# First loads, w_in in parts, whole-batch q and k, and where P is normalised: a reordering of the start of a chunk-attention and gated feed-forward kernel

## The chip, the cores and the metric

The kernel runs on one core of a Trainium2 chip. The metric is the device time of one execution in microseconds (us). The core has a matrix engine (TensorE, PE in the profile, with its weight loads as PEld), a vector engine (VectorE, DVE), a scalar engine (ScalarE, ACT), GpSimd (POOL) and a sync engine (SyncE, SP). Each works through its own queue in program order. Loads and stores are DMAs, issued here from the queues of GpSimd, SP and ACT.

## What is computed

```python
B, H, S, D = 8, 8, 576, 64            # q, k, v: float32
chunk = 64                            # 9 chunks of 64 tokens
scores = (1 / sqrt(D)) * q_c @ k_c^T  # within each chunk
attn = softmax(scores)
attn_out = attn @ v_c
x = attn_out.transpose(0, 2, 1, 3).reshape(4608, 512)
h = x @ w_in                          # 512 x 2048
g = h * sigmoid(beta * h)             # beta: one per column
out = g @ w_out                       # 2048 x 512, float32 out
```

## The kernel before

All matmuls are in float16. Attention goes by **units**: batch 0 (in `WIDE`) has units of 4, 4 and 1 chunks (units 0, 1, 2), every other batch three units of 3 chunks (3 to 23). In one unit, both head halves of all chunks go through: turns of q and k on VectorE (`turn`, 32 x 32 block transposes, L197 and L206), scores on PE (`scores`, L249), row maximum (L261) and subtraction (`shift`, L270) on VectorE, exp on ACT (L278), row sum and reciprocal on VectorE (L289, L293), the product with the reciprocal that makes P (`norm`, L305 and L311), the transposition of P (`flip_pe` L325 with a copy by ACT L333 for the first nine units, `flip_dma` after), P times v on PE (`values`, L353 and L365), and the copy of the result into `XT` (`put`, L376; for units 0 and 1 half on VectorE L386 and half on ACT L384), which holds x transposed, 128 x 4 x 4608.

For units 0 and 1 the loads put 8 tokens of a head in one partition's row, and v is brought into order by matmuls with a selection matrix (`select`, L218; `sel` is made by `make_selectors`, L174 and L178, from an identity made on GpSimd) and copied out of the accumulators by ACT (`select_copy`, L229).

The feed-forward goes by blocks j of 512 tokens: 16 pieces of 128 columns of h (`m_mm`, L399, four matmuls each), tanh on ACT (L411), the gate on VectorE (L417), and then for each 128 tokens 16 matmuls with w_out (`t_mm`, L427), a copy by ACT (L437) and a store (L449, L455). Blocks 0 to 2 take their first step in two parts of tokens (`PIECES`), block 0 in two of 256.

The order of the instructions on every engine is fixed at build time by a planner (L460 to L730): each step is a task with an engine, a length, the tasks it waits for and the buffer slots it takes and gives; the planner puts out whatever can start soonest, feed-forward against attention by small penalties. `order` holds pairs that must keep their order. Loads on GpSimd (`pool`, L498) form one chain in the order of `LOADS` (L485) and then batch by batch; the planner lets one start when its model of the descriptor room (`RING`) has space.

Loads before: q of the first four chunks as float32 by SP and ACT (`load_first`, L137, four DMAs each, cast by VectorE L145 and ACT L143); all else by GpSimd, which casts to float16 on the way. That is k, v of the first four chunks (`load_wide`, L113), the identity, then q, k, v of the next four, w_in in two halves (L163), the first quarter of w_out (L168), the last chunk of batch 0 (`load_last`, L124 and L128), three quarters of w_out, batch 1 by heads in two parts (`load_pair`, L158 for q and k, L153 for v, 8 DMAs each), and the other batches by heads, 8 DMAs for each of q, k and v. P of units 0 to 6 is made on VectorE (`ON_DVE`, L480), of the others on GpSimd.

Of the kernel before, what the change touches and what calls it, by code (L numbers as in the profile page):

```python
# [16 lines left out]
def kernel(  # L17
# [20 lines left out]

    nc = tc.nc
# [9 lines left out]
    WIDE = (0,)  # L49
# [9 lines left out]
    NEARLY = sum(1 for u in units if u[0] in WIDE)  # L59
    first = {b: min(u for u in range(NU) if units[u][0] == b) for b in range(B)}  # L60
# [14 lines left out]
    w_in16 = big.tile([128, 2, KDM, DFF // 2], FP16)  # L75
# [34 lines left out]
    def load_wide(name, b, part):  # L110

        for x in range(2):
            nc.gpsimd.dma_start(  # L113
                out=wide_part(name, b, part)[:, x, :], in_=wide_src(name, b, x, part * 4 * CH))

    def load_last(name, b):

        f = raw_tile(name, b)[:, 2048:2304]
        t0 = 8 * CH
        for x in range(2):  # L120
            if name == "v":
                o = f[64 * x:64 * x + 64].rearrange("p (y s d) -> p y s d", y=2, s=2)
                for y in range(2):
                    nc.gpsimd.dma_start(  # L124
                        out=o[:, y],
                        in_=v[b, 4 * y + 2 * x:4 * y + 2 * x + 2, t0:t0 + CH].rearrange("s p d -> p s d"))
            else:
                nc.gpsimd.dma_start(  # L128
                    out=f[:, 128 * x:128 * x + 128],
                    in_=heads(name, b, x)[:, t0:t0 + CH, :].rearrange("r (p i) d -> r p (i d)", p=32))  # L130
# [15 lines left out]

    def load_pair(name, b, h, c0, n):

        i = srcs[name][b, h, c0 * CH:(c0 + n) * CH]
        if name == "v":  # L150
            p, y, s = 64 * (h // 2 % 2), h // 4, h % 2
            f = raw_tile(name, b).rearrange("p (c y s d) -> p c y s d", c=NCH, y=2, s=2)
            nc.gpsimd.dma_start(  # L153
                out=f[p:p + 64, c0:c0 + n, y, s], in_=i.rearrange("(c p) d -> p c d", p=CH))
        else:
            p, x = 32 * (h // 2), h % 2
            f = raw_tile(name, b).rearrange("p (c x e) -> p c x e", c=NCH, x=2)
            nc.gpsimd.dma_start(  # L158
                out=f[p:p + 32, c0:c0 + n, x], in_=i.rearrange("(c p i) d -> p c (i d)", p=32, i=2))

    def load_w_in(half):
        wv = moe_w_in.rearrange("(kk p) (a f) -> p a kk f", p=128, a=2)
        nc.gpsimd.dma_start(out=w_in16[:, half], in_=wv[:, half])  # L163
# [6 lines left out]
    def make_selectors():  # L170


        for g in range(4):
            nc.vector.tensor_copy(  # L174
                out=diag[32 * g:32 * g + 32], in_=ident[32 * g:32 * g + 32, 32 * g:32 * g + 32])
        for e in range(8):
            for y in range(2):
                nc.vector.tensor_copy(  # L178
                    out=sel[:, y, e].rearrange("p (c k) -> p c k", c=2)[:, :, 8 * e:8 * e + 8],
                    in_=diag[:, 16 * y:16 * y + 16].rearrange("p (c t) -> p c t", c=2))  # L180
# [5 lines left out]
    def turn(name, u, ss=(0, 1)):  # L186
# [3 lines left out]
        if grp is not None:  # L190
            if c0 % 4 == 0:
                f = raw[name, b][:, grp * 1024:grp * 1024 + 1024].bitcast(FP32)
                if 0 in ss:
                    tr[name, b, grp] = tr_p.tile([128, 4, 2, CH, 2], FP16, tag=name + "t", name=name + "t")
# [4 lines left out]
                    in_=f.rearrange("p (s j l) -> p (s j) l", s=2, j=8)[:, 8 * s0:8 * s0 + 8 * n_s])  # L199
            return  # L200
# [25 lines left out]
    def select_copy(b, grp, g):  # L226
        if g == 0:
            tr["v", b, grp] = vv_p.tile([128, 4, 2, 2, D], FP16, tag="vv", name="vv")
        nc.scalar.activation(  # L229
            out=tr["v", b, grp].rearrange("p g y x d -> p g (y x d)")[:, g],  # L230
            in_=sc["v", b, grp][g][:, 0:256], func=ACTF.Copy)
# [7 lines left out]
    def scores(u):  # L239
        n = units[u][2]  # L240
        x = ps_s.tile([128, 2, 512], FP32, tag="s", name="s")
        sc[u] = x
        for c in range(n):
# [53 lines left out]
    def norm(u, gs, eng):  # L297

        n, grp = units[u][2:]
# [8 lines left out]
        else:  # L308
            pn = sm_p.tile([128, m, 2, n, CH], FP16, tag="pn", name="pn")
            for s in range(2):  # L310
                eng.tensor_tensor(  # L311
                    out=pn[:, :, s], in0=ex.rearrange("p g (c s) k -> p s g c k", s=2)[:, s],
                    in1=rb.rearrange("p g (c s) o -> p s g c o", s=2)[:, s].broadcast_to([128, m, n, CH]), op=ALU.mult)
        pr[u, gs] = pn

    def flip_pe(u, gs):
# [6 lines left out]
        f = pn.rearrange("p e g k -> p (e g k)" if grp is None else "p g s c k -> p (g s c k)")  # L323
# [17 lines left out]
    def values(u):  # L341
# [4 lines left out]
        a = ps_x.tile([128, 2, 512], FP32, tag="x", name="xa")  # L346
        if grp is None:
            f = raw["v", b].rearrange("p (c y s d) -> p c y s d", c=NCH, y=2, s=2)
            for c in range(n):
                for y in range(2):  # L350
                    for s in range(2):
                        for g in range(2):
# [3 lines left out]
                                rhs=x[64 * g:64 * g + 64, 2 * c + s, 64 * y:64 * y + 64],  # L356
                                start=True, stop=True)
        else:
            for g in range(2):
                for y in range(2):  # L360
                    for c in range(2):
                        for s in range(2):
                            for r in range(2):
                                o = ((2 * y + g) * 2 + c) * CH
                                nc.tensor.matmul(  # L365
                                    out=a[64 * s:64 * s + 64, r, o:o + CH],
# [5 lines left out]
    def put(u, r=None):  # L372
# [8 lines left out]
        o = XT[:, :, t0:t0 + w].rearrange("p k (c r t) -> p k c r t", c=2, r=2)[:, :, :, r]  # L381
        i = xa[u][:, r].rearrange("p (k c t) -> p k c t", k=KDM, c=2)
# [10 lines left out]
    def m_mm(j, m, a, n):  # L393
# [4 lines left out]
        for kk in range(KDM):  # L398
            nc.tensor.matmul(  # L399
                out=hps[:, 0:n],  # L400
                lhsT=w_in16[:, kg // 2, kk, kg % 2 * 512 + i:kg % 2 * 512 + 512:4],
# [42 lines left out]
    def t_store(j, t):  # L444
# [6 lines left out]
        for i in range(2):  # L451
# [10 lines left out]
            "qt": 3, "kt": 3, "vv": 2}  # L462
# [298 lines left out]
```

## Time and profile before

| what | value |
|---|---|
| median of 3 runs | 318.75 us (318.69 to 320.44) |
| the profiled execution, its own time | 318.93 us |
| its span, first to last instruction | 316.9 us |
| PE, DVE, ACT, POOL busy | 285.8, 207.3, 176.0, 161.7 us |
| feed-forward matmuls L399 and L427 busy | 145.2 and 141.4 us |
| scores L249, transposes L325 busy | 14.6 and 5.3 us |
| P on GpSimd (17 units of 768 columns) | 25.2 us, 1.48 each |
| HBM read, written | 36.71 MB, 9.44 MB |

The profile is one execution. A line of its timeline gives start and length in us, the engine, the line of the kernel, the operation, output and inputs, how many were merged, and in brackets the idle time of that engine just before with what ended it. In a table of stages each engine's busy time stands with its count of instructions, and behind them the clock granted to TensorE as a share of full speed, the mean number of DMA engines' work as a share, and the rate in GB/s of what was written. The page's slices are a fortieth of the span each (7.9 us).

### The profile page before, as it was taken

How to read it: one execution, taken by the hardware profiler on the slowest of the kernel's cores; microseconds unless marked ns; L12 is line 12 of the kernel's file. 1: busy time of each engine (PE TensorE's matmuls, PEld its weight loads, DVE VectorE, ACT ScalarE, POOL GpSimd, SP SyncE). 2: the span in 40 equal slices, each digit the busy share in tenths (PEclk: the TensorE clock that was granted, in tenths of full speed). 3: DMA queues.
4: the chain of work that ended last, by engine and by line, in shares of the span. 5: the costliest groups of instructions: out<-in, count | busy, mean ns of one | idle time of the engine just before them, and what ended most of it. 6: DMA issues, size and time to landing. Idle time of an engine off the chain costs nothing.

```text
span 316.9 us, 7899 instructions
## 1 busy us (share of the span) xinstructions
PE 285.8 (90%) x3254; PEld 165.0 (52%) x3254; DVE 207.3 (65%) x378; ACT 176.0 (56%) x299; POOL 161.7 (51%) x239
## 2 busy tenths in 40 slices
PE   0358787799898999999999999999999999999995
PEld 0347447376684667655455555554444444444442
DVE  3666847589898888978978888887334434334300
ACT  1337455267775777667556866667644454544511
POOL 7624389999999968899689841113000000000000
PEclk9997999999999799999999999999999999999999
DMA  6999948999999999999999963222111000001011
GB/s 100 167 212 131 204 66 71 136 137 129 175 120 155 103 63 125 165 177 131 52 199 147 134 71 85 67 64 48 43 62 41 33 33 35 33 33 68 33 66 66
DMA packets 95315, 31.54 MB, mean 100 GB/s; under 512 B 87600, under 2 KB 88880, under 8 KB 95280
## 3 DMA queue, kind: packets, MB, share of 16 engines
q0 software_dynamic: 77184, 18.12, 60.4%
q10 hardware_dynamic: 5376, 9.70, 9.1%
q1 hardware_dynamic: 12720, 3.22, 7.6%
q8 instruction: 25, 0.41, 0.6%
q14 instruction: 10, 0.08, 0.1%
HBM read 36.71 MB, written 9.44 MB: 146 GB/s over the span
## 4 chain that ended last, share of the span: by engine, by line
PE 75%; DMA 12%; POOL 7%; DVE 2%; ACT 1%; issue 1%; ACTq 0%; DVEq 0%; POOLq 0%
PE hps L399 36%; PE ops L427 35%; DMA w_out<-in_moe_w_out_dram 8%; DMA kr<-in_k_dram 3%; POOL kr L158 3%; PE s L249 3%; PE xa L353 2%; POOL qr L158 2%; POOL vr L153 2%; DVE mx L261 1%; DVE sh L270 1%; POOL w_in L163 0%; PE pt L325 0%; ACT XT L376 0%; ACT osb L437 0%
## 5 line engine op out<-in xcount | busy, mean ns | idle before, releaser
L411 ACT ACTIVATE sg<-hps,beta_sb 128x512 f32<-128x512 f32 (+3 forms) x192 | 108.5, 581 | 77.5 <-PE hps L399 74.9
L399 PE MATMUL hps<-XT,w_in 128*128 128x512 f16 (+3 forms) x768 | 145.2, 332 | 5.7 <-ACT XT L384 2.8
L417 DVE SCALAR_TENSOR_TENSOR gt<-sg,hps 128x512 f16<-128x512 f32 (+3 forms) x192 | 104.8, 551 | 69.7 <-ACT sg L411 67.9
L427 PE MATMUL ops<-w_out,gt 128*128 128x512 f16 x576 | 141.4, 379 | 0.0
L399 PEld LDWEIGHTS <-w_in 128*128 128x128 f16 x768 | 84.6, 115 | 52.7 <-issue 6.3
L427 PEld LDWEIGHTS <-gt 128*128 128x128 f16 x576 | 55.1, 98 | 59.4
L153 POOL DMA_DIRECT2D vr<-in_v_dram x64 | 45.6, 763 | 0.0
L305 POOL TENSOR_TENSOR pn<-ex,ri 128x768 f16<-128x768 f16 x17 | 25.2, 1483 | 35.2 <-ACT sg L411 15.8
L158 POOL DMA_DIRECT2D qr<-in_q_dram x64 | 38.4, 650 | 6.6 <-DMA w_out<-in_moe_w_out_dram 5.8
L158 POOL DMA_DIRECT2D kr<-in_k_dram x64 | 37.9, 623 | 1.9 <-DMA qr<-in_q_dram 1.8
L437 ACT ACTIVATE osb<-ops 128x512 f32<-128x512 f32 x36 | 21.5, 597 | 28.8 <-PE ops L427 28.4
L249 PE MATMUL s<-kt,qt 32*64 32x64 f16 x1152 | 14.6, 197 | 15.2 <-DVE kt L197 10.8
L261 DVE TENSOR_REDUCE mx<-s 128x12 f32<-128x768 f32 (+3 forms) x25 | 22.8, 914 | 7.4 <-PE s L249 7.4
L289 DVE TENSOR_REDUCE sum<-ex 128x12 f32<-128x768 f16 (+3 forms) x25 | 22.5, 901 | 4.3 <-ACT ex L278 4.2
L270 DVE TENSOR_TENSOR sh<-s,mx 128x768 f32<-128x768 f32 (+3 forms) x25 | 22.7, 911 | 0.1
L278 ACT ACTIVATE ex<-sh 128x768 f16<-128x768 f32 (+3 forms) x25 | 20.2, 814 | 2.9 <-issue 0.8
L249 PEld LDWEIGHTS <-qt 32*64 32x64 f16 x1152 | 12.1, 111 | 18.4 <-DVE qt L197 10.1
L376 ACT ACTIVATE XT<-xa 128x768 f16<-128x768 f32 (+1 forms) x22 | 17.2, 782 | 2.4 <-PE xa L353 2.0
L206 DVE STREAM_TRANSPOSE kt<-kr 128x384 f32<-128x384 f32 (+1 forms) x22 | 12.0, 544 | 4.7 <-DMA kr<-in_k_dram 2.9
L333 ACT ACTIVATE et<-pt 128x768 f16<-128x768 f16 (+3 forms) x10 | 7.3, 744 | 10.6 <-PE pt L325 10.2
L206 DVE STREAM_TRANSPOSE qt<-qr 128x384 f32<-128x384 f32 (+1 forms) x22 | 12.0, 550 | 0.4 <-DMA qr<-in_q_dram 0.4
L325 PE MATMUL pt<-ident,pn 128*128 128x128 f16 x54 | 5.3, 232 | 6.4 <-DVE pn L311 4.5
(38 smaller groups left out, 69.6 us busy)
## 6 DMA issues: line engine op xcount, KB each, us to landing
out_dram<-osb ACTq DMA_DIRECT2D x32, 256.0 KB
qr<-in_q_dram POOLq DMA_DIRECT2D x48, 72.0 KB, 4.1
kr<-in_k_dram POOLq DMA_DIRECT2D x48, 72.0 KB, 3.4
vr<-in_v_dram POOLq DMA_DIRECT2D x48, 72.0 KB, 3.3
w_in<-in_moe_w_in_dram POOLq DMA_DIRECT2D x2, 1024.0 KB, 12.4
w_out<-in_moe_w_out_dram POOLq DMA_DIRECT2D x4, 512.0 KB, 9.0
out_dram<-osb ACTq DMA_DIRECT2D x8, 128.0 KB
kr<-in_k_dram POOLq DMA_DIRECT2D x4, 128.0 KB, 7.3
```

The source lines that it names most:

```text
L153: nc.gpsimd.dma_start(out=f[p:p + 64, c0:c0 + n, y, s], in_=i.rearrange("(c p) d -> p c d", p=CH))
L158: nc.gpsimd.dma_start(out=f[p:p + 32, c0:c0 + n, x], in_=i.rearrange("(c p i) d -> p c (i d)", p=32, i=2))
L206: nc.vector.transpose(out=o, in_=f.rearrange("p (e i l) -> p e i l", i=2, l=32))
L249: nc.tensor.matmul(out=x[p0:p0 + 64, r % 2, e:e + CH], lhsT=operand("q", u, r, s, h, c), rhs=operand("k", u, r, s, h, c), start=(h == 0), ...
L261: nc.vector.tensor_reduce(out=mx[:, 0:n].rearrange("p g e o -> p g (e o)"), in_=x[:, gs[0]:gs[-1] + 1, 0:E * CH].rearrange("p g (e k) -> p ...
L270: nc.vector.tensor_tensor(out=sh, in0=x[:, gs[0]:gs[-1] + 1, 0:E * CH].rearrange("p g (e k) -> p g e k", k=CH), in1=mx[:, 0:n].broadcast_t ...
L289: nc.vector.tensor_reduce(out=sm[:, 0:n * E].rearrange("p e o -> p (e o)"), in_=ex.rearrange("p g e k -> p (g e) k"), axis=AX.X, op=ALU.add)
L305: eng.tensor_tensor(out=pn.rearrange("p e g k -> p g e k"), in0=ex, in1=rb.broadcast_to([128, m, 2 * n, CH]), op=ALU.mult)
L399: nc.tensor.matmul(out=hps[:, 0:n], lhsT=w_in16[:, kg // 2, kk, kg % 2 * 512 + i:kg % 2 * 512 + 512:4], rhs=XT[:, kk, tok0:tok0 + n], star ...
L411: nc.scalar.activation(out=sg[:, 0:n], in_=hid[j, m, a][:, 0:n], func=ACTF.Tanh, scale=beta2_sb[:, kg, i:i + 1])
L417: nc.vector.scalar_tensor_tensor(out=gt_tiles[j][:, m, a:a + n], in0=hid.pop(("s", j, m, a))[:, 0:n], scalar=1.0, in1=hid.pop((j, m, a))[: ...
L427: nc.tensor.matmul(out=o, lhsT=gt_tiles[j][:, 4 * kg + i, t * 128:t * 128 + 128], rhs=w_out16[:, kg, i, :], start=(kg == 0 and i == 0), st ...
```

## The change

It does the following:

- `load_first` brings k of the first four chunks as float32 too, by SP and ACT behind their q; both are cast. The table load of ACT's warm-up and the load of beta go behind these.
- GpSimd begins with the identity, the memset of `sel` and the copies of `diag` (VectorE's before), then v of the first four chunks in eight DMAs in place of two.
- The order of loads is new; w_in comes in three tiles of 512, 512 and 1024 columns; q and k of batch 1 come whole, one DMA each, ahead of w_out, and their turn takes the whole batch in two instructions each (`ROWS`, `load_rows`); v stays by heads. The last chunk of batch 0 comes behind w_out, in 12 DMAs in place of 8.
- Two of the four copies of selected v go to VectorE.
- `values` of units 0 and 1 takes two tiles of the pool that the feed-forward uses, one for each engine that copies to `XT`, and P of these units is laid out so that each engine writes 128 tokens that lie together; the copies no longer wait for each other.
- Unit 1 is split in two halves like unit 0; P of all units but unit 0 is made on GpSimd. Pairs in `order` put the steps of the two halves one behind the other, unit 0's values ahead of unit 1's scores and selection, and unit 1's turns behind unit 0's P; the penalty `URGE` favours the steps of units 0 and 1.

```diff
-    WIDE = (0,)
+    WIDE, ROWS = (0,), (1,)
...
-    w_in16 = big.tile([128, 2, KDM, DFF // 2], FP16)
+    w_in_a = big.tile([128, KDM, 512], FP16)
+    w_in_b = big.tile([128, KDM, 512], FP16)
+    w_in_c = big.tile([128, KDM, 1024], FP16)
...
         for x in range(2):
+            if (name, b, part) == ("v", 0, 0):
+                for r in range(4):
+                    nc.gpsimd.dma_start(
+                        out=wide_part(name, b, part)[32 * r:32 * r + 32, x, :], in_=wide_src(name, b, x, 0)[r])
+                continue
...
+    def load_rows(name, b):
+
+        nc.gpsimd.dma_start(
+            out=raw_tile(name, b).rearrange("p (y e) -> p y e", y=2),
+            in_=srcs[name][b].rearrange("(y r) (p j) d -> (r p) y (j d)", y=2, p=32))
...
+    def load_w_in(part):
+        w, c0 = ((w_in_a, 0), (w_in_b, 512), (w_in_c, 1024))[part]
+        nc.gpsimd.dma_start(
+            out=w, in_=moe_w_in.rearrange("(kk p) f -> p kk f", p=128)[:, :, c0:c0 + w.shape[-1]])
...
+        if b in ROWS:
+            if (name, "T", b) not in tr:
+                tr[name, "T", b] = tr_p.tile([128, 2, S, 2], FP16, tag=name + "T", name=name + "T", bufs=1)
+            for y in ss:
+                nc.vector.transpose(
+                    out=tr[name, "T", b][:, y].rearrange("p t h -> p (t h)").bitcast(FP32).rearrange(
+                        "p (t j) -> p j t", j=ROW),
+                    in_=raw[name, b].bitcast(FP32).rearrange("p (y j l) -> p y j l", y=2, j=ROW)[:, y])
+            return
...
+        if g < 2:
+            nc.scalar.activation(out=o, in_=i, func=ACTF.Copy)
+        else:
+            nc.vector.tensor_copy(out=o, in_=i)
...
-            pn = sm_p.tile([128, m, 2, n, CH], FP16, tag="pn", name="pn")
-            for s in range(2):
-                eng.tensor_tensor(
-                    out=pn[:, :, s], in0=ex.rearrange("p g (c s) k -> p s g c k", s=2)[:, s],
-                    in1=rb.rearrange("p g (c s) o -> p s g c o", s=2)[:, s].broadcast_to([128, m, n, CH]), op=ALU.mult)
+            pn = sm_p.tile([128, m, 2, 2, 2, CH], FP16, tag="pn", name="pn")
+            for g in range(m):
+                for s in range(2):
+                    eng.tensor_tensor(
+                        out=pn[:, g, s].rearrange("p y r k -> p r y k"),
+                        in0=ex[:, g].rearrange("p (r y s) k -> p s r y k", r=2, s=2)[:, s],
+                        in1=rb[:, g].rearrange("p (r y s) o -> p s r y o", r=2, s=2)[:, s].broadcast_to([128, 2, 2, CH]),
+                        op=ALU.mult)
...
+            a = [ps_p.tile([128, 512], FP32, tag="p", name="xa") for _ in range(2)]
...
-    ON_DVE = range(0, NEARLY + 4)
-    SPLIT = (0,)
+    ON_DVE = (0,)
+    ORDERS = [[("shift", 0, (0,)), ("max", 0, (1,)), ("shift", 0, (1,)), ("sum", 0, (0,)), ("norm", 0, (0,)), ("sum", 0, (1,))],
+              [("shift", 1, (0,)), ("max", 1, (1,)), ("shift", 1, (1,)), ("sum", 1, (0,)), ("norm", 1, (0,)), ("sum", 1, (1,))]]
+    SPLIT = (0, 1)
+    SPARE = 1
...
+    URGE = 0.8
...
-    LOADS = [("k", 0, 0), ("v", 0, 0), "ident", ("q", 0, 1), ("k", 0, 1), ("v", 0, 1), ("w_in", 0), ("w_in", 1),
-             ("w_out", 0), ("last", "q"), ("last", "k"), ("last", "v"), ("w_out", 1), ("w_out", 2), ("w_out", 3),
-             ("q", 1), ("k", 1), ("v", 1), ("q", 1, 1, 1), ("k", 1, 1, 1), ("v", 1, 1, 1)]
-    PARTS = {1: [(0, 0, 3), (1, 3, 6)]}
+    HEADS = 2
+    TURN = 1.24
+    LOADS = ["ident", ("v", 0, 0), ("q", 0, 1), ("k", 0, 1), ("w_in", 0), ("w_in", 1), ("v", 0, 1), ("w_in", 2),
+             ("q", 1), ("k", 1), ("w_out", 0), ("w_out", 1), ("w_out", 2), ("w_out", 3), ("last", "q"), ("last", "k"), ("last", "v"),
+             ("v", 1, 0), ("v", 1, 1)]
+    V_PARTS = {1: [(0, 3), (3, 6)]}
...
     def load_ident():
         make_identity(nc, ident)
+        nc.gpsimd.memset(sel, 0.0)
+        for g in range(4):
+            nc.gpsimd.tensor_copy(
+                out=diag[32 * g:32 * g + 32], in_=ident[32 * g:32 * g + 32, 32 * g:32 * g + 32])
...
+    for eng, x, length, lag in ((nc.sync, 0, 2.2, 0), (nc.scalar, 1, 2.0, 0)):
+        e = "SP" if x == 0 else "ACT"
+        for name in "qk"[:HEADS]:
+            first_in[name, x] = chain[e] = task(
+                e, length, load_first, eng, name, x, osb_p if name == "q" else sg_p, "osb" if name == "q" else "sg",
+                lag=3.7 if name == "q" else 3.2, behind=chain.get(e))
...
+        if u == 0:
+            order.append((x, selects[0]))
+        if u == 1:
+            order.append((value_of[0], selects[1]))
...
+    order.append((value_of[0], tasks_of[1]))
+    order.append((put_of[0][1], step["max", 1, (0,)]))
+    for x in turned["q", 1] + turned["k", 1]:
+        order.append((step["norm", 0, (1,)], x))
...
+                if x["kind"] == "m" and len(slots["p"]) <= SPARE and tasks[value_of[1]]["end"] is None:
+                    continue
```

The last lines keep one tile of the shared pool free of the feed-forward until unit 1's values are planned. The planner's model of the descriptor room now keeps count for four groups of DMA engines.

## The prediction

> **What bounds the kernel now.** I read the page first (busy shares, slices), then stages of the span, then the timeline of the first 48 us and GpSimd's own timeline.
>
> ```profile
> PE 285.8 (90%) x3254; PEld 165.0 (52%) x3254; DVE 207.3 (65%) x378; ACT 176.0 (56%) x299; POOL 161.7 (51%) x239
> ...
> PEclk9997999999999799999999999999999999999999
> DMA  6999948999999999999999963222111000001011
> ```
>
> PE is busy 285.8 of 316.9 us, so only some 31 us of idle time can be won, and a part of the slow-clock time. The stages say where the idle time lies (columns: stretch, its length, busy time of PE, PEld, DVE, ACT, POOL; then granted clock, DMA share, GB/s):
>
> ```profile
> 0.00:24.25 24.25, 7.52 (x296) 6.37 (x297) 14.14 (x44) 7.57 (x17) 13.66 (x25) 1.00 1.02 161
> ...
> 24.25:66.20 41.95, 34.34 (x388) 23.35 (x387) 27.55 (x58) 21.71 (x44) 32.33 (x56) 0.96 0.96 120
> 66.20:103.16 36.96, 33.75 (x530) 24.90 (x529) 33.29 (x63) 25.24 (x49) 36.21 (x57) 1.00 1.43 145
> 103.16:313.30 210.14, 210.14 (x2046) 110.40 (x2045) 132.30 (x215) 120.87 (x189) 79.53 (x103) 0.99 0.61 81
> 313.30:316.90 3.60, 0.03 (x1) 0.00 (x0) 0.00 (x0) 0.60 (x1) 0.00 (x0) 1.00 0.19 73
> ```
>
> PE idles 16.7 us before the first feed-forward matmul, 7.6 until block 0 is done at 66.2, 3.2 until 103, then not at all, and 3.6 in the last copy and store. A microsecond of idle time saved before 103 us moves the end by as much, since all behind it is solid PE work. A change of loads and early order can touch the first three: 27.5 us. The start, from the timeline:
>
> ```profile
> 18.38 1.89 PE L218 MATMUL va<-vr,sel 32*128 32x128 f16 x64
> ...
> 20.20 0.61 PE L325 MATMUL pt<-ident,pn 128*128 128x128 f16 x4
> ...
> 20.74 0.94 PE L249 MATMUL s<-kt,qt 32*64 32x64 f16 x64
> ...
> 21.75 1.23 DVE L261 TENSOR_REDUCE mx<-s 128x16 f32<-128x1024 f32 x1 [2.46 <-PE s L249]
> 22.89 0.68 DVE L386 CAST XT<-xa 128x512 f16<-128x512 f32 x1
> ...
> 23.60 0.60 ACT L384 ACTIVATE XT<-xa 128x512 f16<-128x512 f32 x1 [1.33 <-DVE XT L386]
> 24.25 7.07 PE L399 MATMUL hps<-XT,w_in 128*128 128x256 f16 x48 [2.04 <-ACT XT L384]
> ```
>
> The first unit's scores start at 10.75, its XT is whole at 24.2: 13.5 us, in which unit 1's selection, scores and row maximum stand ahead of unit 0's flips, values and copies. Then GpSimd, which issues the loads in order:
>
> ```profile
> 26.15 0.58 POOL L124 DMA_DIRECT2D vr<-in_v_dram  x1 [4.39 <-DMA w_in<-in_moe_w_in_dram]
> ...
> 38.04 0.56 POOL L158 DMA_DIRECT2D qr<-in_q_dram  x1 [2.93 <-DMA w_out<-in_moe_w_out_dram]
> ...
> 41.13 4.43 POOL L158 DMA_DIRECT2D kr<-in_k_dram  x8
> ```
>
> It stands still while big loads drain, then issues batch 1 piece by piece from 30.8 to 64.4 us. PE pays at 49.29 (2.06 us) and 62.65 (1.81 us), both waits for batch 1's turned k.
>
> **First q, k as float32.** SP and ACT each issue eight loads in place of four. The q issues end at 2.55, so four more of 0.39 to 0.45 end at 4.3. Low bound for k: 4.3 plus the shortest issue-to-landing of any q load, 2.0, is 6.3. High bound: before, the last q was issued at 2.52 and cast at 8.98, 6.4 later; 4.3 + 6.4 = 10.7. That slow case had GpSimd's loads on the engines from about 3 us on; now the first of these is issued only behind the identity (0.22 + 0.29), the memset of the selectors (0.91 on VectorE; 3.6 if the 0.22 for 128 columns scales) and four copies of 0.1 to 0.3, at 3.1 to 6.6 us. So I lean to the low end: 7.6. Then cast 0.59, turn 0.40, handing over 0.2: scores at 8.8 (7.5 to 11.9) instead of 10.75. ACT's table load goes behind its eight issues to 4.35 and is over, with the warm-up, at 5.9, ahead of the data; if q landed at 5 it would cost 0.9.
>
> **Unit 0's chain.** By the added order VectorE does max, shift, max, shift, sum, norm, sum, norm without the turns of q (0.70) between: 0.69 + 0.68 + 0.69 + 0.68 + 0.86 + 0.82 + 0.86 + 0.82 = 6.1, from 1.34 after the scores start. Two copies of selected v come to VectorE: 0.78 at ACT's 0.39, which I count whole, though off the chain ACT loses as much and the first exp no longer stands 1 us behind four of them. Then flip 0.61, copy 0.60, values 0.45, XT 0.68 on both engines side by side now (own tiles), and four hand-overs, 0.35: 1.34 + 6.1 + 0.8 + 2.7 = 10.9. First feed-forward matmul at 8.8 + 10.9 = 19.7 instead of 24.25. But unit 1's selection and scores (1.89 + 0.94 = 2.83) have to be done behind it, so the net is 4.55 - 2.83 = 1.7 us won (low end 3.0 won, high end 1.4 lost).
>
> **w_in in three parts, and its place.** The first MB (512 columns) has to be there at 19.7. Ahead of it are three 0.26 MB loads (written bytes) instead of five, and 0.52 instead of 1.05 MB of its own: 1.05 MB less, 5 us at the 208 GB/s of the stage from 14 to 27 us; GpSimd starts 1.9 to 5.4 later. The view of w_in has its two halves land 10.3 and 14.5 after their issues; the first so at 10.62 + 10.3 = 20.9, so the new one at 17.8 to 21.3: about in time. The last 1024 columns follow v's second part: 0.26 MB less ahead than the old second half (11.39 + 14.5 = 25.9), 1.3 us, against the late start, of which I take 2: 26.6. PE reaches them after 8 x 0.43 = 3.4, with a half-clock window 1.7 more: 24.8. A wait of 2 us, between 0 and 4.
>
> **Unit 1** now splits in halves and normalises on GpSimd. Scores at 20; VectorE 4.5, last half on GpSimd 0.98 (1.48 x 512/768), flip, copy, values, XT and hand-overs 3.1: 28.6, with eight gates of 0.42 between, 32. PE needs it at 19.7 + 6.9 + 1.7 + 2 + 2.8 = 33.1, so it is just hidden; before, its XT was whole at 40.4. Each microsecond lost beyond 1 is PE idle time.
>
> **Batch 1's q, k whole, ahead of w_out.** 32 issues of 0.56 (17.9) become two, at w_in's 0.77 (1.5): 16.4 less for GpSimd. Added there: six issues for the first v (3.5), four for the last chunk (2.4), one for w_in (0.8), identity work (1.3 to 4.8), and P of units 1 to 6: 1024, 256 and four times 768 columns at 1.48 for 768, 8.4. So its busy time is about even; what goes is waiting (10.1 for v, 5.8 for q), as two big loads drain with no issue behind. 1.18 MB (written) at 200 GB/s is 5.9: both are in by 33, and w_out by some 42 instead of 40.3, when PE is still in block 0's first half (33.1 + 7 + attention). Units 2 and up wait for the last chunk, now behind w_out (44), and v of batch 1 (16 x 0.62 behind it, 54); PE has block 0's output matmuls (16 x 0.86) until about 58. Both k waits, 3.9 us, go. Their turns become four of 576 columns: 0.84 each by columns from 0.56 for 384, 1.24 if the wide stride of the output costs what the planner's TURN says; 3.4 to 5.0 instead of 3.3, hidden while VectorE has the 9 us of slack of 42 that the stage shows.
>
> **P on GpSimd, later units.** Frees VectorE of 0.93 a unit; GpSimd is 0.55 slower a piece and in order behind bursts of eight issues (4.5 to 5.9). Hidden where a unit is a block ahead; where not, like the 1.25 us at 102.36 that PE waited for it already.
>
> **Stage sums.** 24 to 66: of 7.6 idle, 3.9 (k) go and 2.4 (first gates and XT) are replaced by the w_in wait of 2; 1.5 others stay: 3.5, 4.1 won (0 to 6). 66 to 103: loads run 6 to 10 us earlier; 3.2 becomes 1.5, 1.7 won (-1 to 3.2).
>
> **Clock.** The stretches 24.79:28.20 and 103.29:106.71 ran at 0.50, each behind a stretch of the same length in which PE was busy 1.30 and 1.87 of 3.4 us. Each costs 1.7. The second may go with the idle time, and the wait for w_in may make another: I count none (1.7 either way). The Trainium skill, TensorE: Matmul & The Clock Gate, Part 1, has the clock halved only after a whole idle window; by that the second would not be due, and once gone the time would be 1.7 less, 309.7. The trace disagrees: PE was busy over half of the window ahead of it.
>
> **Sum.** 1.7 + 4.1 + 1.7 = 7.5. The profiled execution took 318.93 (span 316.9 and 2.0 around it; median 318.75): 311.4, 2.3% less.
>
> **Rivals.** *All closes*: low end at the start (3.0), 5.6 in block 0, 2.7 behind, one half-clock window less (1.7): 13.0, 305.9. For it: GpSimd's waits, the bound of all supply, mostly go. Against: the first 256 tokens still need every step of the chain. Chance 0.15.
>
> *Loads no earlier at the start*: GpSimd's loads slow SP's and ACT's as before (the first q came 6.4 us after its last issue), k lands at 10.7, w_in's third part slips by 3 more, as GpSimd starts late. 311.4 + 3.1 + 3.0 = 317.5, within 1%. For it: the DMA share is 0.9 and more from slice 2 on. Against: 266 GB/s at 2 to 3 us, before GpSimd's packets. Chance 0.16. The Trainium skill, DMA: Bandwidth & Descriptors, Issuing engines are not separate DMA queues, says that another issuer saves only issue time; by it k keeps its 9.5, scores start at 10.5 and the time is 313.1.
>
> *P stuck on GpSimd* (slower): the halves of unit 1, then units 2 and 3, queue behind a load that waits for room; the waits were 3.80 and 4.39 us. Two for unit 1 cost 8.2 less the slack of 1, and 4.5 for a burst ahead of units 2 and 3: 311.4 + 7.2 + 4.5 = 323. It decides where unit 1's XT is later than 40.4, its old place: no gain; 44 means over 1% lost. For it: GpSimd stood still for 18 us of the first 41. Against: the planner places P among the loads by when it expects room. Chance 0.12.
>
> Forecast as summed: 0.57, with a range of its own of 308 to 315. A measurement here tells about 1% from no change. Faster by over 1% (under 315.6): 0.57 + 0.15 = 0.72; within 1%: 0.16; slower: 0.12. The range 305.5 to 318 leaves out the last rival and a little of the others.
>
> **What would show it.** Scores near 8.8 and the first L399 near 19.7; no L249 wait for a turned k of batch 1; one load each for q and k of batch 1; PE idle before L399's second half of w_in near 2 us; unit 1's XT by 33; GpSimd's batch 2 at 54 to 58 instead of 64.4. Wrong if PE waits for P on GpSimd, for w_out, or if block 0 ends later than 60 us.

## The result, and the profile after

The changed kernel takes 322.51 us (median of 8 runs, 321.30 to 322.78) where the kernel before took 318.72 (8 runs) beside it: a ratio of 1.0099, 95% interval 1.0070 to 1.0128. It is 1% slower. The profiled execution took 322.49, its span is 320.7.

The page, by the same rows as before:

```profile
PE 287.4 (90%) x3254; PEld 164.6 (51%) x3254; DVE 204.9 (64%) x373; ACT 177.1 (55%) x298; POOL 160.9 (50%) x232
...
PEclk9999999999999999999999999999999999999999
DMA  6799967689797997999599999922201000001111
```

PE is busy 1.6 us longer than before with the same 3254 instructions, so of the 3.8 us that the span grew, 2.2 are idle time. Where that lies, by stages (columns as before):

```profile
0.00:20.11 20.11, 6.13 (x232) 4.77 (x232) 12.49 (x41) 6.34 (x12) 15.80 (x31) 1.00 0.81 135
20.11:24.00 3.89, 3.60 (x16) 2.27 (x16) 3.75 (x8) 2.24 (x5) 1.07 (x2) 1.00 1.24 196
24.00:37.00 13.00, 0.80 (x9) 0.35 (x13) 1.42 (x5) 0.47 (x1) 4.37 (x8) 1.00 1.11 214
37.00:66.00 29.00, 29.00 (x384) 20.99 (x385) 22.45 (x46) 18.07 (x39) 18.16 (x31) 1.00 0.77 98
66.00:103.00 37.00, 34.49 (x482) 23.90 (x480) 29.69 (x58) 25.68 (x50) 31.52 (x44) 1.00 0.99 107
```

The first feed-forward matmul starts at 20.11 instead of 24.25, and PE is not idle from 37 to 66. But from 24 to 37 PE works 0.80 of 13 us, VectorE 1.42 and ScalarE 0.47, while the DMA engines are busy throughout. In the kernel before, PE worked 10.53 us of the same stretch:

```profile
24.00:37.00 13.00, 10.53 (x77) 8.48 (x77) 9.77 (x22) 8.25 (x18) 6.14 (x11) 0.87 1.04 164
```

The timeline of PE in the changed kernel:

```profile
9.25 1.07 PE L291 MATMUL s<-kt,qt 32*64 32x64 f16 x64 [9.25 <-DVE kt L211]
...
20.11 3.60 PE L448 MATMUL hps<-XT,w_in_a 128*128 128x256 f16 x16 [0.54 <-DMA w_in_a<-in_moe_w_in_dram]
36.02 0.39 PE L371 MATMUL pt<-ident,pn 128*128 128x128 f16 x2 [12.30 <-POOL pn L355]
...
39.14 1.06 PE L448 MATMUL hps<-XT,w_in_b 128*128 128x256 f16 x4
```

For 12.30 us PE waits to transpose unit 1's P, which GpSimd makes (L355). VectorE's part of it, the last reciprocal, was done at 24.1:

```profile
23.88 0.20 DVE L335 RECIPROCAL ri<-sum 128x8 f32<-128x8 f32 x1
```

GpSimd's own timeline tells why P comes only at 35.34:

```profile
20.36 0.54 POOL L185 DMA_DIRECT2D w_out<-in_moe_w_out_dram  x1 [1.96 <-DMA w_in_a<-in_moe_w_in_dram]
22.96 0.53 POOL L185 DMA_DIRECT2D w_out<-in_moe_w_out_dram  x1 [2.06 <-DMA w_in_b<-in_moe_w_in_dram]
24.34 0.53 POOL L185 DMA_DIRECT2D w_out<-in_moe_w_out_dram  x1 [0.85 <-DMA vr<-in_v_dram]
24.86 0.56 POOL L137 DMA_DIRECT2D qr<-in_q_dram  x1
29.17 0.56 POOL L137 DMA_DIRECT2D qr<-in_q_dram  x1 [3.75 <-DMA w_in_c<-in_moe_w_in_dram]
31.95 0.54 POOL L137 DMA_DIRECT2D qr<-in_q_dram  x1 [2.22 <-DMA qr<-in_q_dram]
34.74 0.54 POOL L137 DMA_DIRECT2D qr<-in_q_dram  x1 [2.26 <-DMA kr<-in_k_dram]
35.34 2.34 POOL L355 TENSOR_TENSOR pn<-ex,ri 128x256 f16<-128x256 f16 x4
```

P stands in order behind four loads of the last chunk's q, and three of these wait, 8.2 us together, for something that they have no use for: the landing of w_in's third part, then of batch 1's whole q, then of its whole k. Counting the loads on this queue from the start shows the pattern: the load that ends its wait is always the eighth before. The last chunk's q are loads 24 to 27; w_in_c is 17, whole q 18, whole k 19; likewise w_out's second and third (21, 22) wait for w_in_a and w_in_b (13, 14). The trace's records of waits agree for each of the first 51: the program has eight semaphores (counters by which a landed load releases whoever waits for it) for these loads, in rotation, and load n waits on the one that load n - 8 raises. So no more than eight loads of this queue are under way at once; this limit lies in the program's own waits, and whether the queue would hold more isn't shown. The planner knew nothing of that: it modelled room for descriptors and put these loads at 20.9 to 22.9, without a gap, with P right behind.

The Trainium skill, DMA: Bandwidth & Descriptors, Why a DMA increments its semaphore by 16 and not by 1, asks for one semaphore per transfer in flight, since two that share one can fill each other's count. Eight semaphores that must not be shared are then eight transfers in flight; that GpSimd stands still on them is what the rows above show, at 2.2 to 3.8 us for each of the three loads.

### The profile page after: what moved, and what is told of

It reads as the page before. It is cut to its first block, busy times and chain, and to the rows that moved or that the text cites. A ratio compares the mean times of both kernels' runs of the same rounds, so it can differ in the third digit from the quotient of the medians.

```text
span 320.7 us, 7900 instructions
## 1 busy us (share of the span) xinstructions
PE 287.4 (90%) x3254; PEld 164.6 (51%) x3254; DVE 204.9 (64%) x373; ACT 177.1 (55%) x298; POOL 160.9 (50%) x232
## 2 busy tenths in 40 slices
DMA packets 88452, 31.80 MB, mean 99 GB/s; under 512 B 79712, under 2 KB 81760, under 8 KB 88416
## 4 chain that ended last, share of the span: by engine, by line
PE 77%; DMA 8%; DVE 5%; POOL 3%; ACT 3%; issue 2%; ACTq 1%; DVEq 0%; POOLq 0%
PE hps L448 36%; PE ops L476 35%; DMA qr<-in_q_dram 7%; PE s L291 3%; DVE gt L466 2%; PE xa L399 2%; ACT sg L460 2%; DVE sum L331 1%; POOL vr L122 1%; DMA vr<-in_v_dram 1%; ACTq L504 1%; PE pt L371 1%; PE va L241 1%; ACT osb L486 1%; POOL sel L589 1%
## 5 line engine op out<-in xcount | busy, mean ns | idle before, releaser
L448 PE MATMUL hps<-XT,w_in_c 128*128 128x512 f16 (+3 forms) x384 | 71.3, 326 | 0.8 <-DVE gt L466 0.3
L448 PEld LDWEIGHTS <-w_in_c 128*128 128x128 f16 x384 | 41.8, 113 | 23.1 <-issue 1.5
L348 POOL TENSOR_TENSOR pn<-ex,ri 128x768 f16<-128x768 f16 (+1 forms) x22 | 31.5, 1434 | 39.0 <-DVE ri L335 16.7
L448 PE MATMUL hps<-XT,w_in_a 128*128 128x512 f16 (+3 forms) x192 | 38.6, 339 | 0.5 <-DMA w_in_a<-in_moe_w_in_dram 0.5
L448 PE MATMUL hps<-XT,w_in_b 128*128 128x512 f16 (+3 forms) x192 | 37.5, 335 | 1.1 <-DVE gt L466 0.8
L448 PEld LDWEIGHTS <-w_in_b 128*128 128x128 f16 x192 | 21.4, 115 | 13.2 <-issue 1.5
L448 PEld LDWEIGHTS <-w_in_a 128*128 128x128 f16 x192 | 21.2, 117 | 13.1 <-DMA w_in_a<-in_moe_w_in_dram 0.7
L303 DVE TENSOR_REDUCE mx<-s 128x12 f32<-128x768 f32 (+2 forms) x26 | 23.0, 883 | 6.3 <-PE s L291 5.0
L331 DVE TENSOR_REDUCE sum<-ex 128x12 f32<-128x768 f16 (+2 forms) x26 | 22.7, 875 | 3.0 <-ACT ex L320 3.0
L312 DVE TENSOR_TENSOR sh<-s,mx 128x768 f32<-128x768 f32 (+2 forms) x26 | 22.9, 881 | 0.3
L371 PE MATMUL pt<-ident,pn 128*128 128x128 f16 x54 | 6.1, 244 | 16.3 <-POOL pn L355 12.5
```

Source lines behind the costliest of these rows:

```text
L303: nc.vector.tensor_reduce(out=mx[:, 0:n].rearrange("p g e o -> p g (e o)"), in_=x[:, gs[0]:gs[-1] + 1, 0:E * CH].rearrange("p g (e k) -> p ...
L312: nc.vector.tensor_tensor(out=sh, in0=x[:, gs[0]:gs[-1] + 1, 0:E * CH].rearrange("p g (e k) -> p g e k", k=CH), in1=mx[:, 0:n].broadcast_t ...
L331: nc.vector.tensor_reduce(out=sm[:, 0:n * E].rearrange("p e o -> p (e o)"), in_=ex.rearrange("p g e k -> p (g e) k"), axis=AX.X, op=ALU.add)
L348: eng.tensor_tensor(out=pn.rearrange("p e g k -> p g e k"), in0=ex, in1=rb.broadcast_to([128, m, 2 * n, CH]), op=ALU.mult)
L448: nc.tensor.matmul(out=hps[:, 0:n], lhsT=(w_in_a, w_in_b, w_in_c, w_in_c)[kg][:, kk, 512 * (kg // 3) + i:512 * (kg // 3) + 512:4], rhs=XT[ ...
```

## The experiments

*Theory*: the forecast's gains are there, and P on GpSimd, in order behind loads that wait for the eighth load before them, takes them back and more. *Rivals*: VectorE or the clock eats the gains; descriptor room and not a count of loads holds the queue; it is only unit 1's place in the order; or PE would have stood from 24 to 37 in any case, as w_in's third part and w_out land late (supply). Ratios are to the kernel before, run beside each; runs 1 to 4 were on one chip, 5, 8, 9 and 12 on a second, 6, 7, 10 and 11 on a third. In runs 3, 10 and 11 the order of all else stays as it was. In every other run the planner made a new order with the edit, so the time holds the new order's worth too.

**1. P of unit 1 on VectorE.**

```diff
-    ON_DVE = (0,)
+    ON_DVE = (0, 1)
```

> The changed kernel with P of unit 1 on VectorE (as P of unit 0), nothing else. Theory A (queue position): P of unit 1 stands on GpSimd's queue behind four loads of the last chunk, each of which waits for the landing of the eighth load before it, and PE stands 12.3 us for it; with P on VectorE it is ready by 26, PE's idle time from 24 to 37 us falls from 12.2 to 2 to 4, and the time from 322.5 to 313.5 (311 to 316). Rival (supply): the third part of w_in landed only at 29 and w_out at 39 to 45, so PE would have stood anyway: 319 to 322.

Measured: 322.08 us, 1.0108 (1.0066 to 1.0150). The wait went, and PE was busy 11.41 of the 13 us from 24 to 37, so supply didn't hold it there; but the time stayed. GpSimd and PE, later:

```profile
47.45 10.22 POOL L174 DMA_DIRECT2D vr<-in_v_dram  x16
57.73 0.61 POOL L348 TENSOR_TENSOR pn<-ex,ri 128x256 f16<-128x256 f16 x1
```

```profile
58.40 0.40 PE L371 MATMUL pt<-ident,pn 128*128 128x128 f16 x2 [5.05 <-POOL pn L348]
```

Now unit 2's P stands behind batch 1's sixteen loads of v. These wait for nothing; 16 issues of 0.64 are enough. The granted clock was 0.79 from 50 to 66 and 0.91 from 66 to 103, and PE's busy time rose by 4.7 to 292.1. I had expected the time to fall to 313.5 with the first wait. Of the 10.6 us of idle time that went from 24 to 37, 5.0 came back from 50 to 66 and 2.6 elsewhere, and the longer busy time took more than what was left. The profiled execution, at 324.24, is 2.2 above the median, so its sum isn't the median's.

**2. The same P ahead of the last chunk's loads**, still on GpSimd.

```diff
+    order.append((step["norm", 1, (1,)], last_of[0]))
```

> The changed kernel with P of unit 1 still on GpSimd, but put ahead of the loads of the last chunk. Theory A: P starts behind w_out's fourth load at about 24.9 and is done at 27.3; time 314.5 (312 to 317), a microsecond or so behind the run with P on VectorE. Rival (GpSimd as such, its slower arithmetic or its sharing with the loads): P still late, over 320.

Measured: 318.49, 0.9973 (0.9942 to 1.0004): neither expectation held. PE's waits for P:

```profile
PE pt L371 <- POOL pn L348: 5.5, 1, 5.5
...
PE pt L371 <- POOL pn L355: 2.8, 2, 2.5
```

12.5 us for unit 1 became 2.8, and 5.5 for unit 2 stand there now: the gain is 4 us, where run 5, without any of these waits, will gain 13. The place in the order matters, but one place is not the whole cause. In the edit, `last_of` holds the last chunk's loads.

**3. w_out in one load of 2 MB** instead of four of 0.5, at the place of the first. The bytes and packets stay (88404 packets, 88452 before the edit); only the count of loads falls.

```diff
-        nc.gpsimd.dma_start(out=w_out16.rearrange("p kg i f -> p kg (i f)")[:, kg], in_=wv[:, kg])
+        if kg == 0:
+            nc.gpsimd.dma_start(out=w_out16.rearrange("p kg i f -> p kg (i f)"), in_=wv)
```

> The changed kernel with w_out brought by one load instead of four, at the place of the first; same bytes, same planned order. Theory A (a load waits for the landing of the eighth before it): the four loads of the last chunk's q now wait for w_in's first two parts and v's second part, landed by 24.3, not for w_in's third part, q and k of batch 1; P of unit 1 starts by 25.5 instead of 35.3 and the time is 314.5 (312 to 318). Rival (room for descriptors, as the planner models it): the same descriptors wait as before, P starts at 35 and the time stays at 322.5 within 1.

Measured: 319.41, 0.9987 (0.9957 to 1.0017), above theory A's range. With three loads fewer, unit 1's P came at 25.67 instead of 35.34, as a limit on the count of loads has it and one on descriptors has not. GpSimd:

```profile
24.55 1.06 POOL L137 DMA_DIRECT2D qr<-in_q_dram  x2 [0.27 <-DMA vr<-in_v_dram]
25.67 2.34 POOL L356 TENSOR_TENSOR pn<-ex,ri 128x256 f16<-128x256 f16 x4
...
44.69 0.54 POOL L137 DMA_DIRECT2D kr<-in_k_dram  x1 [9.19 <-DMA w_out<-in_moe_w_out_dram]
```

The last row is the eighth load behind w_out, which now waits 9.19 for all of it; and PE waited 5.1 us for w_out, all of which now has to land before its first part is used. So the total says little, the rows say which limit it is.

**4. Only P on GpSimd, in the kernel before.**

```diff
-    ON_DVE = range(0, NEARLY + 4)
+    ON_DVE = (0,)
```

> The kernel before with one part of the change alone: P of units 1 to 6 on GpSimd. Theory A: P of unit 1 falls behind batch 1's loads on GpSimd's queue, to 44 us or later instead of 35.3 to 36.5, and PE stands for it: 325 to 330. Rival (which engine makes P does not matter, as GpSimd has time): 318 to 320.

Measured: 325.79, 1.0206 (1.0123 to 1.0288), within theory A's range. PE's waits:

```profile
PE pt L325 <- POOL pn L311: 8.0, 2, 7.4
```

These 8.0 us are for unit 1's P. This part alone costs some 2% with the old order of loads too.

**5. All of the change but P on GpSimd.**

```diff
-    ON_DVE = (0,)
+    ON_DVE = range(0, NEARLY + 4)
```

> The changed kernel without its part on P: VectorE normalises P of units 0 to 6 again, as before the change; loads, parts of w_in and turns as changed. Theory A (the change's gains are there, and only P on GpSimd, waiting behind loads that wait for the eighth load before them, takes them back): no wait of PE for P over 1 us, PE idle under 3 us in 24-37 and under 2 us in 50-66, total 309 to 314 us, faster than before by 1.5 to 3%. Theory B (VectorE, with units 1 and 2's P again, closes XT late): PE idle in 20-66 stays at 6 us or more, for VectorE, total 316 to 320. Theory C (what the first 24 us win is lost again to the clock): PE idle as in A, but more than 2 us of busy time more than before's, total 314 to 318.

Measured: 309.27 us (309.19 to 309.96), 0.9724 (0.9683 to 0.9764). It beats both kernels, as the theory has it, and the first rival falls: PE's busy time is 285.3, before's 285.8, and unit 1's XT is whole at 30.8 with VectorE making its P. (Up to 23.6 us its column of the clock is no reading, see the last section.) The stages:

```profile
0.00:20.11 20.11, 6.21 (x232) 4.89 (x232) 12.05 (x41) 6.34 (x12) 15.78 (x31) 1.00 0.79 135
20.11:24.00 3.89, 2.75 (x12) 1.62 (x12) 3.75 (x8) 2.35 (x5) 1.07 (x2) 1.00 1.24 197
24.00:37.00 13.00, 11.73 (x172) 9.98 (x173) 10.21 (x26) 9.18 (x21) 2.71 (x5) 0.87 1.10 213
37.00:66.00 29.00, 27.34 (x358) 18.57 (x357) 24.02 (x46) 16.46 (x35) 22.52 (x37) 1.00 1.04 130
66.00:103.00 37.00, 36.58 (x569) 26.27 (x567) 34.34 (x65) 27.21 (x51) 36.09 (x54) 1.00 1.36 140
```

Against the changed kernel's stages the 13.3 us between the spans (320.7 and 307.4) come out whole: idle time from 24 to 37 fell by 10.9, from 66 to 103 by 2.1, behind that by 0.6, PE's busy time by 2.2; idle time grew by 0.8 before 24 and by 1.7 from 37 to 66. This order too was planned anew, and no run takes P off GpSimd in the changed kernel's very order. So how much of the 13.3 us is the order isn't shown; what the rows show is that the wait of 12.3 us for P is gone.

**6. P of units 0, 1 and 2 on VectorE**, 3 to 6 on GpSimd.

```diff
-    ON_DVE = (0,)
+    ON_DVE = (0, 1, 2)
```

> The changed kernel with P of units 0, 1 and 2 on VectorE, of units 3 to 6 on GpSimd. With only units 0 and 1 on VectorE the time was 322.1, with units 0 to 6 309.3. Theory A (unit 2 is what waits, behind the second batch's sixteen loads of v; the later units are early): PE waits for P on GpSimd under 2 us, total 310 to 313. Theory B (each unit's P stands behind whichever loads come next, and the wait moves on to units 3 to 6): a wait of 3 us or more for P on GpSimd between 55 and 103 us, total 315 to 320.

Measured: 321.35, 1.0055 (1.0029 to 1.0082), above theory B's range. Its mechanism is there: the wait moved on to unit 3, behind the next batch's loads. GpSimd, then PE:

```profile
47.62 10.24 POOL L174 DMA_DIRECT2D vr<-in_v_dram  x16
57.77 4.29 POOL L166 DMA_DIRECT2D qr<-in_q_dram  x7
62.13 1.47 POOL L348 TENSOR_TENSOR pn<-ex,ri 128x768 f16<-128x768 f16 x1
```

```profile
63.66 0.82 PE L371 MATMUL pt<-ident,pn 128*128 128x128 f16 x6 [5.41 <-POOL pn L348]
```

Taking unit 1, or units 1 and 2, off GpSimd won almost nothing (322.1 and 321.4); taking off 3 to 6 as well won 10.5 by the ratios, 12.1 by the medians. GpSimd works without a gap from 45 to 77 us, and the first unit that comes to it there pays about 5.

**7. The changed kernel, planned with the true limit**: a load starts when the eighth before it has landed.

```diff
-                    t = room_at(t, x["load"][2])[0]
+                    need = len(landed) + loads_of(x) - 8
+                    t = max([t] + landed[max(0, need - 1):max(0, need)])
```

> The changed kernel as it is, P of units 1 to 6 on GpSimd, but the order planned with the rule that a load can start only when the eighth load before it has landed, in place of the room for descriptors. Theory A (the loss is the planner's wrong picture of the loads; P on GpSimd is no evil in itself): the planner puts unit 1's P ahead of the last chunk's loads, PE's waits for P on GpSimd shrink from 12.5 to under 4 us, total 311 to 315. Theory B (GpSimd has too much to issue in the first 70 us, however it is ordered): unit 1's P comes early, but unit 2's or a later one's stands behind loads, or the loads behind P; 5 us or more of waits remain, total 316 to 321.

Measured: 315.79, 0.9895 (0.9842 to 0.9949). The lines that fill `landed` and `loads_of` are left out above. The planner by itself put unit 1's P ahead of the last chunk's loads, at 26.02, and the waits fell from 12.5 to 2.7:

```profile
26.02 2.34 POOL L355 TENSOR_TENSOR pn<-ex,ri 128x256 f16<-128x256 f16 x4 [1.54 <-DVE ri L335]
...
48.54 10.23 POOL L174 DMA_DIRECT2D vr<-in_v_dram  x16
58.72 2.12 POOL L348 TENSOR_TENSOR pn<-ex,ri 128x256 f16<-128x256 f16 x2
```

The time lies between what the theories gave, 0.8 above A's range: the order by the right picture of the loads wins back about half of what run 5 wins (2.0 of 3.75%, from 1.0099 to 0.9895, run 5 being at 0.9724). The other half this order doesn't remove: unit 2's P is still made behind the sixteen loads of v, at 58.72, and PE idles 4.4 us from 50 to 66.

**8. Both: that rule, and P of units 0 to 6 on VectorE.**

> The same with the planner told that a load on GpSimd can start only when the eighth load before it has landed, in place of its room for descriptors; the program's order is planned again by it. Theory A: if P is off GpSimd nothing that PE waits for stands behind the loads, so the order changes little: within 1% of the run with P on VectorE alone. Rival: the loads themselves (w_out, second batch's v) still come late behind their eighth load, and an order planned by the true rule wins 1% or more.

Measured: 311.02, 0.9773 (0.9733 to 0.9813), 0.6% more than run 5. With P off the queue the better picture wins nothing: theory A.

**9. Run 5 with the first k as FP16 by GpSimd**, planned anew (`HEADS = 1`, k first in `LOADS`).

> The run with P of units 0 to 6 on VectorE, but with the first k loaded as FP16 by GpSimd's queue again instead of as float32 with two casts on VectorE: the first part of the change undone alone. Theory A: first scores come at 10 us or later instead of near 9.2, the first feed-forward matmul 1 to 2 us later, and the total is 1 to 2 us (0.3 to 0.6%) longer than that run. Rival: the first feed-forward matmul is set by w_in's first part or VectorE's chain, not by k; total the same within 0.3%.

Measured: 318.92, 1.0024 (1.0003 to 1.0045): 9.6 us more than run 5, where both theories gave 2 at most. Neither holds. VectorE and PE at 66 us:

```profile
69.92 0.58 DVE L229 STREAM_TRANSPOSE qt<-qr 128x384 f32<-128x384 f32 x1 [4.75 <-DMA kr<-in_k_dram]
```

```profile
70.86 1.86 PE L448 MATMUL hps<-XT,w_in_b 128*128 128x256 f16 x8 [4.93 <-DVE gt L466]
```

A turn that waits for a load stands on VectorE ahead of a gate that is ready, and PE waits for the gate. That is the new order, not the start. So:

**10. The same edit in run 5's very order** (the planner sees run 5's steps; only what the three of them put out differs).

```diff
+        if name == "k":
+            return
...
     def load_ident():
+        load_wide("k", 0, 0)
```

The first pair of lines stands in `load_first` and in `cast_first`.

> The run with P of units 0 to 6 on VectorE (309.3), in its very order, but the first k loaded as FP16 by GpSimd's queue, ahead of the identity, instead of as float32 with a cast each on VectorE and ScalarE. Undoing this together with a newly planned order gave 318.9. Theory A: the part itself is worth 1 to 2 us (first scores at 9.1 to 10.2 instead of 9.2, first feed-forward matmul some 1.3 us later), and the rest of those 9.6 us was the order: total 310.3 to 311.5. Rival: the two loads more on GpSimd's queue push the later ones back through the eighth load before them, and the time is 314 or more in the same order.

Measured: 313.37, 0.9813 (0.9753 to 0.9872). Run 5 was at 309.27 and 0.9724 on another chip: the first part of the change is worth 2.8 us by the ratios, 4.1 by the medians, between my two expectations, and 5.5 to 6.8 of the 9.6 us were the order. PE's start in this run:

```profile
10.29 1.07 PE L294 MATMUL s<-kt,qt 32*64 32x64 f16 x64 [10.29 <-DVE kt L214]
...
22.21 2.75 PE L451 MATMUL hps<-XT,w_in_a 128*128 128x256 f16 x12 [0.60 <-DMA w_in_a<-in_moe_w_in_dram]
...
40.37 1.04 PE L479 MATMUL ops<-w_out,gt 128*128 128x512 f16 x4 [0.95 <-DMA w_out<-in_moe_w_out_dram]
```

2.0 us are the first feed-forward matmul (22.21 for 20.20), 0.95 is a wait for w_out, which comes later on the queue; PE's busy time is 1.1 more.

**11. Run 5 with w_in in two halves**, in its very order.

```diff
-        w, c0 = ((w_in_a, 0), (w_in_b, 512), (w_in_c, 1024))[part]
+        if part == 2:
+            return
+        w, c0 = ((w_in_a, 0), (w_in_c, 1024))[part]
```

> The same run in its very order, but w_in in two halves: the first at the place of the first part, the second at that of the second part, none at the third's. Theory A: the first feed-forward matmul, which had its part 0.3 us late, waits for a load twice as large, 0.5 MB of FP16 more at some 200 GB/s: 2.5 us, total 311 to 313. Rival: the first half is there by the time XT is, or the waits behind it get shorter by as much (its third part no longer follows), total within 0.5% of 309.3.

Measured: 310.85, 0.9739 (0.9685 to 0.9793): 0.5 us more than run 5 by the ratios, 1.6 by the medians, which the intervals can't tell from nothing. The wait is as theory A expected, the time as its rival did:

```profile
PE hps L449 <- DMA w_in_a<-in_moe_w_in_dram: 2.4, 1, 2.4
```

It cost less than its length: PE's busy time is run 5's within 0.1 us, but from 37 to 50 PE is not idle at all, where run 5 idles 1.3.

**12. Run 5 with w_out ahead of batch 1's q and k**, planned anew.

> The run with P of units 0 to 6 on VectorE, but with w_out's four loads ahead of the second batch's whole q and k, as before the change: that move undone alone. Theory A: PE waits again for the second batch's turned k near 50 to 66 us, 2 to 5 us in all, total 1 to 2% longer than that run. Rival: q and k land in time behind w_out too (w_out is 2 MB as float32 and could land by 45 us), total within 0.5%, and the move is worth nothing once the loads are few.

Measured: 314.39, 0.9884 (0.9836 to 0.9933), 5.1 us more. (w_out has 2 MB as float16, and 4 MB as float32.) The time is theory A's, its mechanism isn't: once the first scores have started, no matmul waits over 0.3 us for a turned k. Batch 1's first scores come at 54.25 instead of 51.17, PE idles 3.4 from 50 to 66 in waits for several engines, and PE is busy 2.1 longer, with a granted clock of 0.95 from 50 to 66. As run 9 shows, an order planned anew can cost as much by itself, so what this move is worth is left open; it wasn't tried in run 5's order.

## Why the prediction was wrong

*The step that failed* is "Unit 1", which "normalises on GpSimd" with "last half on GpSimd 0.98", "so it is just hidden". Its XT was to be whole by 32 and was whole at 41.5:

```profile
40.86 0.69 DVE L435 CAST XT<-xa 128x512 f16<-128x512 f32 x1 [1.22 <-PE xa L414]
```

The length of P was not far off: two pieces of 0.61 make 1.2 for a half. What was left out is the queue in front of them, 11.3 us from 24.1 to 35.34. The prediction shows that GpSimd "issues the loads in order" and stands still for 2.9 and 4.4 us at loads; it drew from that when the loads land, not when P behind them is made. "Hidden where a unit is a block ahead" failed in the same way for units 2 and 3 in runs 1 and 6 (5.0 and 5.4 us behind bursts of issues); in the changed kernel itself PE didn't wait for them, since unit 1 had held it up already. The prediction had named the sign: "Wrong if PE waits for P on GpSimd".

A second step let the wait cost PE its whole length. The prediction had PE at work on block 0's first half until it needs unit 1's XT at 33.1. But the transposition of unit 1's P stands in PE's order behind only 16 of that half's 64 matmuls. So PE stood from 23.7 on, though w_in's second part had landed by 22.96 (GpSimd's wait for it ends there); its first matmuls came at 39.14, behind the transposition. What another order on PE would have saved was not tried.

*The rival that names it*, "P stuck on GpSimd", gave 323 for the 322.5 measured; it had 0.12. That the number came so near is partly luck. Its price was 11.7 us: two waits of 8.2 together for unit 1, and 4.5 for a burst ahead of units 2 and 3. There were three waits, of 8.2 together, and the burst cost PE nothing here; PE's one wait was 12.3, as the issues of w_out's last load and of the four loads of q stand in that queue too. Beside the 13.3 between the changed kernel's span and run 5's the price was 1.6 too small, and run 5 is 2.1 below the forecast: the two errors nearly cancel. It decided by unit 1's XT: no gain at 40.4, 1% lost at 44. At the measured 41.5 1% was lost already, for PE idles 2.5 us from 66 to 103 where 1.5 were forecast, and is busy 1.6 longer where nothing was counted. The reason given, "a load that waits for room", was wrong: what is short is not room, the eighth load before is still under way. The waits in the profile before end on the eighth load too (its loads of the last chunk's v wait for w_in's two halves); counting loads would have shown three waits ahead of P.

*The rest of the sum* can be read from run 5, which is the change without that step, in its own order: 309.3, forecast 311.4. Idle time before the first feed-forward matmul fell by 2.8 (1.7 forecast; scores at 9.2, 8.8 forecast; the matmul at 20.2, 19.7 forecast), from there to 66.2 by 3.6 (4.1), from there to 103.16 by 2.8 (1.7), and busy time by 0.5 (nothing): 9.7 instead of 7.5, less 0.2 of idle time behind. In the forecast's sum for 24 to 66, the parts (3.9, 2.4 and 1.5) add up to 7.8, where the stage has 7.6 idle; 0.2 us of that 4.1 are too few.

- "First q, k as float32", counted within the 1.7: right in mechanism, and worth some 3 to 4 in all (run 10), as loads further down the queue move up too.
- "w_in in three parts", a wait of 2 us for the third part: there is none; the first part is 0.3 to 0.5 late instead. As one of two halves it would be 2.4 late (run 11), which cost 0.5 to 1.6.
- "Batch 1's q, k whole": the two k waits, 3.9 us, went. What is left of such waits is 0.5 in the changed kernel, none of it for batch 1, and 1.2 in run 5, for batch 0's last chunk. GpSimd was to reach batch 2's loads at 54 to 58: 57.6 in run 5, 61.8 in the changed kernel.
- "Clock: none counted": the busy time, which a slower clock lengthens, is 0.5 less in run 5, near it, and 1.6 more in the changed kernel.
- *All closes* (305.9) and *Loads no earlier at the start* (317.5) are both refuted, the first by run 5's sum, the second by the changed kernel's own start: k was turned and the scores began at 9.25, not at 10.5 or later.

## What to carry to other kernels

A calculation that is put on a queue of loads can cost the queue ahead of it and not only its own length: before placing it there, list what is issued ahead of it and, for each load, which earlier load it waits for (here the eighth before), and take the landing of the biggest. Splitting a small load into more pieces uses up places in flight, and the piece behind then waits for a large load that it has nothing to do with. Where a planner writes the order, an edit tried alone is tried in a new order too; hold the order fixed to price the edit (run 9 against run 10: 9.6 against 4.1 us by the medians). Run 5, the main one here, was not held fixed.

## What the runs showed of the hardware

- GpSimd issues loads and calculates in one order: a load that waits for the landing of another holds up the P behind it. Waits of up to 9.19 us (run 3) were for a load that the waiting one doesn't use, by the program's rotation of eight semaphores, whatever the loads' sizes.
- The first feed-forward matmuls took twice as long as later ones, under a row of the granted clock that reads 1.00. In the changed kernel 16 of 256 columns took 3.60 us at 20.11, 0.225 each; 20 of the same form took 2.35 at 42.83, 0.118 each:

```profile
42.83 2.35 PE L448 MATMUL hps<-XT,w_in_c 128*128 128x256 f16 x20
```

  That 1.00 is no reading. The changed kernel's trace holds no record of the clock before 42.4 us, where the first one, full speed, begins, and the row counts a stretch without a record as 1.00. Run 5's records begin at 23.6, those of run 11 at 32.2; the first record is full speed in every run here. The Trainium skill, TensorE: Matmul & The Clock Gate, Part 1, has half speed as the state of an idle array that some 3.4 us of work release. The first matmuls here, with PE busy 6.13 of the 20.11 us ahead of them, agree with half speed (0.225 against 0.118). The Trainium skill also warns there that the gate's events in traces are not always reliable. Here the durations of matmuls of one form tell the speed where the row cannot.
